# Moving six of eight chunks of one half row's upper partitions onto the lower ones, in a two-layer decode step

## The chip, the cores and the metric

The kernel runs on one core of one Trainium2 chip. Its engines are TensorE (PE in the profile; PEld is its weight load), VectorE (DVE), ScalarE (ACT), GpSimd (POOL) and SyncE (SP). Data is moved by sixteen DMA engines that all queues share. The metric is the time of one execution in microseconds, the median of several runs, on the device.

## What is computed

Two decode layers are run twice over a batch of 2 with one new token each: attention over a cache, then a gated MLP, each behind a layer norm and with a residual.

```python
def _A_ref(x, k_cache, v_cache, wq, wo):
    q = (x @ wq).reshape(B, Sq, H, Dh)...
    scores = jnp.einsum("bhqd,bhkd->bhqk", q, k_cache) * (Dh ** -0.5)
    o = jnp.einsum("bhqk,bhkd->bhqd", softmax(scores), v_cache)
    return o... @ wo
def _B_ref(x, w_gate, w_up, w_down):
    g = jnp.einsum("bsd,df->bsf", x, w_gate)
    u = jnp.einsum("bsd,df->bsf", x, w_up)
    return jnp.einsum("bsf,fd->bsd", _gelu(g) * u, w_down)

x = A_x
x = x + _A_ref(_layernorm(x), A_k_cache, A_v_cache, A_wq, A_wo)
x = x + _B_ref(_layernorm(x), B_w_gate, B_w_up, B_w_down)
x = x + _A_ref(_layernorm(x), A_k_cache, A_v_cache, A_wq, A_wo)
x = x + _B_ref(_layernorm(x), B_w_gate, B_w_up, B_w_down)
```

The batch is 2, the model width D is 576, there are 32 heads of 128 with a cache of 8192 positions, and the MLP width DF is 4608. Everything is float32.

## The kernel before

**Space.** One tile, `space` (line 133), holds 50,176 floats in each of 128 partitions. Nearly all that is loaded goes there: cache parts, and the rows of the weights. A small planner, `Arena` (lines 68 to 119), gives out ranges of it while the program is written: `slots` and `pair` for cache parts, `ring` for pieces of fixed size, and `fit` (line 107) for any width, at the first free place from where the last one ended.

**Order of the loads.** `plan_first`, `plan_mlp` and `plan_second` (lines 324 to 412) put every load into one list, `queue`, in the order in which the work will need them. `pump` (line 148) issues from the head of the list as long as the planner has room. `done` (line 152) frees a range after the last instruction that reads it and pumps again. So loads are written into the program as early as room allows, all on SP's queue (`nc.sync.dma_start`), and the tile framework adds the semaphore waits: for the instructions that last read the range, and for earlier transfers. Transfers take one of eight completion semaphores in turn.

**Order of the engines.** The instructions of each engine stand in the order in which the Python code calls them (`manual_schedule`, line 131). Between engines only the semaphores decide.

**Attention.** Each layer reads 64 pairs of batch and head. VectorE multiplies keys with the query (line 644), GpSimd adds halves (line 661), VectorE reduces (line 664), ScalarE takes the exponential (line 721), and TensorE multiplies with the values (line 762). At the end `project` (lines 807 to 817) multiplies eight groups of wo's rows, one after another as they land; a group has 16 matmuls, for 4 rows and 4 column strips. `add_to_x` (line 520) adds the result to x.

**The second MLP.** `norm` (line 486) centres x and transposes it into `xt`, in which each of nine 32-column blocks holds the 128 entries that belong to one block of weight rows. The gate and up matrices have 576 rows of 4608; each row is cut into two half rows of 2304, which gives 1152 half rows, nine for each of the 128 partitions. `half_rows` (line 221) loads some of the nine for all partitions in one transfer: three transfers of three for gate, then two of three and three of one for up (`GU`, line 305). Row and half fall on partitions so that even and odd partitions hold the two halves.

`all_products` (line 959) multiplies them in that order. For each of the nine there are eight matmuls: the 2304 columns are eight chunks of 288 (HG), of which chunk (v, c) is added up in strip c (32 partitions) of half v of `acc`. `window` (line 938) is the 8-column slice of `xt` that serves as the left operand.

Then `activate` (line 973) works on each half v in turn: a scaled copy on ScalarE (line 976), a transpose, and the GELU and product with up on VectorE and ScalarE, into `hT`. Last come the down products (line 1004): 36 rows per partition, loaded in eight transfers (`down`, line 264), each transfer's products following `IDLE` idle matmuls (`idle_products`, line 524), which compute nothing that is used. `add_to_x` and two stores (line 1019) end the kernel.

Of the kernel before, what the change touches and what calls it, by code (L numbers as in the profile page):

```python
# [9 lines left out]
F32 = mybir.dt.float32  # L10
# [5 lines left out]
P = 128  # L16
B = 2
# [8 lines left out]
HALF = P // 2  # L26

GH = 4
NU = 9
EQ = 512  # L30
HG = DF // 16
PAD = 6
# [9 lines left out]
RING = 5 * SLOT  # L42
END = RING + NPLACE * PLACE
HELD = 5


class Item:
# [75 lines left out]
def decode_layers(ctx, tc, x_in, kc, vc, wq, wo, wg, wu, wd, out):  # L123
    nc = tc.nc
    scale = DH ** -0.5

    consts = ctx.enter_context(tc.tile_pool(name="consts", bufs=1))
# [18 lines left out]
    queue, ready, places = [], {}, {}  # L146

    def pump():
        while queue and queue[0]():
            queue.pop(0)  # L150

    def done(key):
        arena.free(key)
        pump()

    def part_at(at, n):
        return space[:, at:at + n]
# [51 lines left out]
    def weights(key, n, first, transfers):  # L209

        def make():
            at = arena.ring(key, n) if first is None else arena.fit(key, n, first)
            if at is None:
                return False
            t = ready[key] = part_at(at, n)
            transfers(t)
            return True

        queue.append(make)

    def half_rows(key, w, us, first):

        width = w.shape[1] // 2
        rows = w.rearrange("r (s w) -> (r s) w", w=width).rearrange("(p u) w -> p u w", p=P)

        def transfers(t):
            nc.sync.dma_start(t.rearrange("p (u w) -> p u w", w=width), rows[:, us[0]:us[-1] + 1, :])

        weights(key, len(us) * width, first, transfers)

    def of_half(h, k):

        width = wq.shape[1] // 2
        rows = wq.rearrange("r (s w) -> (r s) w", w=width).rearrange("(p u) w -> p u w", p=P)

        def transfers(t):
            for e in range(2):
                nc.sync.dma_start(t[e::2, :], rows[e::2, 2 * k + (h + e) % 2, :])

        weights(("wq", 1, h, k), width, None, transfers)  # L240

    def split_rows(name, w, h, u):

        rows = w[:, DF // 2 * h:DF // 2 * (h + 1)].rearrange("(m r) w -> m r w", r=NU)

        def transfers(t):
            for e in range(2):
                nc.sync.dma_start(t[e::2, :], rows[:, 5 * e + u, :])

        weights((name, 0, h, u), DF // 2, None, transfers)  # L250

    def split_middle(h):

        def transfers(t):
            for g, w in enumerate((wg, wu)):
                for e in range(2):
                    lo, n = DF // 4 * (2 * h + e), DF // 4
                    nc.sync.dma_start(
                        t[e::2, n * g:n * (g + 1)], w[:, lo:lo + n].rearrange("(m r) w -> m r w", r=NU)[:, 4, :]
                    )  # L260

        weights(("gu", 0, h), DF // 2, None, transfers)
# [136 lines left out]
    def plan_mlp(layer):  # L399
        if layer == 0:  # L400
            for h in range(2):
                for u in range(4):
                    split_rows("g", wg, h, u)
                split_middle(h)
                for u in range(4):
                    split_rows("u", wu, h, u)
        else:
            for g, (name, w) in enumerate((("g", wg), ("u", wu))):
                for us in GU[g]:
                    half_rows((name, layer, us[0]), w, us, 0)  # L410
        for rows in DOWN[layer]:
            down(layer, rows)

    plan_first()
    plan_mlp(0)
    plan_second()
    plan_mlp(1)
    pump()


    ident = consts.tile([P, P], F32, name="ident")
# [27 lines left out]
    side = consts.tile([P, 2], F32, name="side")  # L449
# [9 lines left out]

    xt = consts.tile([P, PAD + NU * 32], F32, name="xt")
    nc.vector.memset(xt, 0.0)


    acc = psum1.tile([P, 2, 512], F32, name="acc")
# [13 lines left out]
    def small(p, n):  # L480

        smalls.append(smalls.pop(0))
        return smalls[0][0:p, 0:n]
# [36 lines left out]
    def add_to_x():  # L520
        nc.vector.tensor_add(x, xps, x)  # L521
# [409 lines left out]
    def mlp(layer):  # L931
        split = layer == 0
        rstd = norm(split)
        if split:
            idle_products(3)
        hT = once.tile([P, 2, NI, 2, 2, B], F32, name="hT", tag="xc")

        def window(u, at):

            return xt[:, PAD + 32 * u - at:PAD + 32 * u - at + 4 * B]  # L940

        def split_products(h):

            steps = [(("g", layer, h, u), u, 2, (0,)) for u in range(4)] + [(("gu", layer, h), 4, 1, (0, 1))]
            steps += [(("u", layer, h, u), u, 2, (1,)) for u in range(4)]
            for key, u, sides, gs in steps:
                w = ready.pop(key).rearrange("p (k c w) -> p k c w", c=4, w=HG)
                for k in range(2):
                    g, e = (k, 0) if u == 4 else (gs[0], k)
                    for c in range(4):  # L950
                        nc.tensor.matmul(
                            acc[32 * c:32 * c + 4 * B, h, :HG], window(u, 4 * g + 2 * e), w[:, k, c, :],
                            start=(key == steps[0][0] and k == 0), stop=(key == steps[-1][0] and k == 1),
                        )
                done(key)
                if key != steps[-1][0]:
                    idle_products(1)

        def all_products():

            for g, name in enumerate("gu"):
                for us in GU[g]:
                    w = ready.pop((name, layer, us[0])).rearrange("p (u v c w) -> p u v c w", v=2, c=4, w=HG)
                    for u in us:
                        for v in range(2):
                            for c in range(4):
                                nc.tensor.matmul(
                                    acc[32 * c:32 * c + 4 * B, v, :HG], window(u, 4 * g), w[:, u - us[0], v, c, :],
                                    start=(g == 0 and u == 0), stop=(g == 1 and u == NU - 1),
                                )  # L970
                    done((name, layer, us[0]))

        def activate(v):

            o = once.tile([P, 2, HG], F32, name="o", tag="row")
            nc.scalar.activation(o[:, 0, :], acc[:, v, :HG], AF.Copy, scale=rstd)  # L976
            gu = o[:, 1, :].rearrange("p (i r) -> p i r", i=NI)
            nc.vector.transpose(gu, o[:, 0, :].rearrange("p (m i) -> p i m", i=NI))  # L978
            g = gu[:, :, 0:4]
            a = once.tile([P, NI, 4], F32, name="ga", tag="part")  # L980
            nc.vector.tensor_mul(a, g, g)
            nc.vector.tensor_scalar(a, a, 0.044715, 1.0, op0=ALU.mult, op1=ALU.add)
            nc.vector.tensor_mul(a, a, g)
            nc.scalar.activation(a, a, AF.Tanh, scale=math.sqrt(2.0 / math.pi))
            nc.vector.scalar_tensor_tensor(a, a, 1.0, g, op0=ALU.add, op1=ALU.mult)
            nc.vector.tensor_mul(a, a, gu[:, :, 4:8])
            a, to = a.rearrange("p i (e b) -> p (i e) b", b=B), hT[:, v].rearrange("p i e s b -> p (i e) s b")
            nc.vector.tensor_scalar_mul(to[:, :, 0, :], a, 0.5)
            nc.scalar.mul(to[:, :, 1, :], a, 0.5)

        if not split:
            all_products()
        for v in range(2):
            if split:
                split_products(v)
            activate(v)
        for n, rows in enumerate(DOWN[layer]):
            if n < len(IDLE[layer]):
                idle_products(IDLE[layer][n])
            w = ready.pop(("d", layer, rows[0])).rearrange("p (i c) -> p i c", c=D)  # L1000
            for k, (t, i) in enumerate(rows):
                v, e = divmod(t, 2) if split else (t % 2, t // 2)
                for c in range(4):
                    nc.tensor.matmul(  # L1004
                        xps[32 * c:32 * c + 2 * B, :], hT[:, v, i, e, :, :].rearrange("p s b -> p (s b)"),
                        w[:, k, c * CW:(c + 1) * CW],
                        start=(rows is DOWN[layer][0] and k == 0), stop=(t, i) == (NT - 1, NI - 1),
                    )
            done(("d", layer, rows[0]))
        add_to_x()  # L1010
        if layer == 0:
            idle_products(1)
# [34 lines left out]
```

## Time and profile before

| | |
|---|---|
| time, median of 3 runs | 2686.63 us (2686.4 to 2686.9) |
| profiled execution, first to last instruction | 2685.0 us |
| loaded from memory | 1153.18 MB, 429 GB/s over the span |
| DVE busy | 1806.0 us (67%) |
| POOL busy | 1161.8 us (43%) |
| PE busy | 914.4 us (34%) |
| ACT busy | 163.7 us (6%) |

The profile is of one execution, taken by the hardware. Its page has the busy time of each engine, forty slices of the span with the share of the DMA engines and the clock that TensorE was granted, the DMA queues, the chain of waits that ended last, and the costliest groups of instructions. A row of the timeline has the start and the length in us, the engine, the line of the kernel, the operation, the tile that it writes and those it reads, the shape, the count, and in brackets the idle time ahead of it with what ended that. A matmul in float32 stands in the rows as two instructions. An engine's name with a q is its sequencer, which issues transfers and waits.

### The profile page before, as it was taken

The numbers are of one execution on the slowest core, as the hardware profiler recorded it, in microseconds if no ns is written. First come the engines' busy times: TensorE is split into PE (matmuls) and PEld (weight loads), VectorE is DVE, ScalarE is ACT, GpSimd is POOL, SyncE is SP. The second block draws the span as 40 slices with busy tenths as digits, with TensorE's granted clock in tenths as the row PEclk, the third lists the DMA queues.
The fourth block names the chain that finished last, engine by engine and source line by source line (L and its number), as shares of the span: only waits on it lengthen the run. The fifth ranks groups of instructions, "written<-read, shape, count | busy, mean of one in ns | idle before, by whom it ended". The sixth has DMA issues, their size and how long they took to land. (4 is left out here: it accounts for less than half of the span.)

```text
span 2685.0 us, 17174 instructions
## 1 busy us (share of the span) xinstructions
PE 914.4 (34%) x7150; PEld 305.4 (11%) x7150; DVE 1806.0 (67%) x874; ACT 163.7 (6%) x786; POOL 1161.8 (43%) x261
## 2 busy tenths in 40 slices
PE   1323332332233233334663333233223323332356
PEld 0100010010001000111221101001000100010022
DVE  4876687677667766867037877667766776776640
ACT  0000000000000000000026000000000000000000
POOL 2543454354445444544028455445444543454420
PEclk7656666665666566566986665666566656656678
DMA  9999999999999999999999999999999999999998
GB/s 422 436 436 426 437 432 434 433 434 432 433 431 435 436 428 433 436 428 425 414 418 434 431 431 436 431 434 434 437 428 434 434 435 431 431 434 435 433 421 375
DMA packets 33950, 1154.30 MB, mean 430 GB/s; under 512 B 4152, under 2 KB 4176, under 8 KB 5968
## 3 DMA queue, kind: packets, MB, share of 16 engines
q1 hardware_dynamic: 33832, 1153.19, 99.8%
q8 instruction: 56, 0.92, 0.1%
q14 instruction: 22, 0.18, 0.0%
q10 hardware_dynamic: 40, 0.01, 0.0%
HBM read 1153.18 MB, written 0.00 MB: 429 GB/s over the span
## 5 line engine op out<-in xcount | busy, mean ns | idle before, releaser
L661 POOL TENSOR_TENSOR space<-space 128x3072 f32<-128x3072 f32 (+3 forms) x221 | 1128.6, 5107 | 1263.3 <-DVE space L644 1202.5
L644 DVE TENSOR_TENSOR space<-space,bank 128x6144 f32<-128x6144 f32 (+3 forms) x223 | 1112.7, 4991 | 560.2 <-DMA space<-in_A_k_cache_dram 496.8
L762 PE MATMUL acc<-space,prz 128*8 128x512 f32 x4096 | 594.6, 744 | 199.4 <-DMA space<-in_A_v_cache_dram 195.5
L664 DVE TENSOR_REDUCE S<-space 128x48 f32<-128x3072 f32 (+3 forms) x223 | 569.3, 2553 | 89.9 <-POOL space L661 89.6
L592 PE MATMUL bank<-qsb,pick 4*64 4x128 f32 (+1 forms) x256 | 46.3, 436 | 863.1 <-DVE space L644 853.1
L762 PEld LDWEIGHTS acc<-space,prz 128*8 128x8 f32 x4096 | 119.1, 104 | 616.3 <-issue 410.6
L784 PE MATMUL bank<-of,osb 128*32 128x2 f32 x512 | 40.9, 202 | 324.4 <-DVE osb L777 324.4
L713 ACT ACTIVATE nbs<-bank 128x2 f32<-128x2 f32 (+1 forms) x68 | 11.6, 171 | 1848.2 <-PE bank L698 1801.8
L592 PEld LDWEIGHTS bank<-qsb,pick 4*64 4x64 f32 (+1 forms) x256 | 20.7, 202 | 882.5 <-DVE space L644 863.2
L517 POOL TENSOR_TENSOR rstd<-ve,mhalf 128x1 f32<-128x1 f32 x4 | 2.2, 550 | 168.8 <-DVE ve L515 168.8
L690 PE MATMUL bank<-ident,m 128*1 128x128 f32 x68 | 19.5, 286 | 160.7 <-DVE m L688 160.5
L784 PEld LDWEIGHTS bank<-of,osb 128*32 128x32 f32 x512 | 35.9, 154 | 331.7 <-DVE osb L777 330.5
L978 DVE STREAM_TRANSPOSE o<-o 128x288 f32<-128x288 f32 x4 | 2.8, 691 | 94.5 <-ACT o L976 94.5
L729 PE MATMUL bank<-sums,unit 128*128 128x2 f32 x120 | 35.2, 363 | 87.0 <-ACT prz L721 87.0
L776 DVE TENSOR_TENSOR acc<-acc,diag 128x512 f32<-128x512 f32 x64 | 43.5, 680 | 22.0 <-PE acc L762 22.0
L721 ACT ACTIVATE prz<-S,nbs 64x128 f32<-64x128 f32 (+1 forms) x128 | 50.7, 396 | 17.3 <-POOL prz L711 14.4
L803 ACT ACTIVATE oT<-bank,rinv 32x8 f32<-32x8 f32 x110 | 28.5, 259 | 381.5 <-PE bank L784 380.8
L654 ACT ACTIVATE space<-space 128x128 f32<-128x128 f32 x164 | 48.3, 296 | 23.6 <-DVE space L644 21.7
L698 PE MATMUL bank<-m,unit 1*128 1x2 f32 (+1 forms) x136 | 39.0, 354 | 25.3 <-DVE m L696 25.3
L777 DVE TENSOR_REDUCE osb<-acc 128x128 f32<-128x512 f32 x64 | 44.3, 691 | 2.2
L521 DVE TENSOR_TENSOR x<-bank,x 128x144 f32<-128x144 f32 x4 | 1.2, 308 | 64.1 <-PE bank L1004 40.4
L729 PEld LDWEIGHTS bank<-sums,unit 128*128 128x128 f32 x120 | 30.1, 311 | 92.2 <-ACT prz L721 92.2
(73 smaller groups left out, 427.6 us busy)
## 6 DMA issues: line engine op xcount, KB each, us to landing
space<-in_A_v_cache_dram SPq DMA_DIRECT2D x8, 4096.0 KB
space<-in_A_k_cache_dram SPq DMA_DIRECT2D x6, 4096.0 KB
space<-in_A_wo_dram SPq DMA_DIRECT2D x15, 1152.0 KB
space<-in_A_k_cache_dram SPq DMA_DIRECT2D x15, 1024.0 KB
space<-in_B_w_down_dram SPq DMA_DIRECT2D x9, 1152.0 KB
space<-in_B_w_gate_dram SPq DMA_DIRECT2D x3, 3456.0 KB
space<-in_A_v_cache_dram SPq DMA_DIRECT2D x10, 1024.0 KB
space<-in_A_wq_dram SPq DMA_DIRECT2D x3, 3072.0 KB
```

Of the source, the lines that this page charges most:

```text
L592: nc.tensor.matmul(qb[n][to, :], pick[32 * c:32 * c + 4, r:r + 1].to_broadcast([4, P // it.heads]), qsb[32 * c:32 * c + 4, (h % 4) * DH:(h ...
L644: nc.vector.tensor_tensor(out=u[:, :rows, :], in0=t[:, :rows, :], in1=qb[n].unsqueeze(1).to_broadcast([P, rows, DH]), op=ALU.mult)
L654: nc.scalar.activation(u[:, j, :], u[:, j, :], AF.Copy, accum_out=S[n][:, k * JC + j:k * JC + j + 1])
L661: nc.gpsimd.tensor_tensor(out=half, in0=half, in1=u[:, :r, DH // 2:], op=ALU.add)
L664: nc.vector.tensor_reduce(out=S[n][:, k * JC:k * JC + own_rows(n, k, m)], in_=prod.pop((n, k)), axis=AX.X, op=ALU.add)
L698: nc.tensor.matmul(mT[n][:, :heads], ones[0:1, :], m1[:, :heads], start=True, stop=True)
L721: nc.scalar.activation(pr[at, lo:].rearrange("p (g e) -> p g e", e=4)[:, 0:it.rows // 2:2, :], s[at, :it.rows].rearrange("p (g r) -> p g r ...
L729: nc.tensor.matmul(tot[n][:, :ITEMS[n].heads], ones, rs.pop(n), start=True, stop=True)
L762: nc.tensor.matmul(accumulator(n)[32 * c:32 * c + 8, :], pr[:, at:at + 8], t[g // 4][:, g % 4 * 4:g % 4 * 4 + 4, :].rearrange("p j d -> p ...
L776: nc.vector.tensor_tensor(out=q, in0=q, in1=diag.unsqueeze(2).to_broadcast([P, 4, DH]), op=ALU.mult)
L777: nc.vector.tensor_reduce(out=t, in_=q.rearrange("p r d -> p d r"), axis=AX.X, op=ALU.add)
L784: nc.tensor.matmul(po[lo:lo + 32, i, :], t[:, i::GH], of, start=True, stop=True)
```

## The change

Of the second MLP's up matrix, the ninth half row of each partition is loaded and multiplied in another way.

- `lower_rows` replaces `half_rows` for it. One transfer loads the last two chunks (576 columns) for all 128 partitions. The first six chunks (1728 columns, CUT = 6) are loaded by eight transfers, each to eight of the lower 64 partitions, four apart. Each brings two runs per partition: the partition's own, and that of the partition 64 above it. The second run lies 4 columns further on than the first one's end. The place in `space` is 4040 columns wide; before it was 2304.
- `move_down` copies the upper partitions' block of `xt` for this half row down to the lower ones: a matmul with a part of the identity, and a copy on ScalarE into four new columns at the end of `xt`. It is called ahead of all products.
- `last_products` replaces the eight matmuls of the ninth up half row. Each of the first six chunks is multiplied in two matmuls over the lower 64 partitions, one for each run; the last two chunks as before over all 128.

```diff
+CUT = 6
...
+    def lower_rows(key, w, u, cut, first):
+
+        width = w.shape[1] // 2
+        rows = w.rearrange("r (s w) -> (r s) w", w=width).rearrange("(q u) w -> q u w", u=NU)[:, u, :]
+        moved = rows.rearrange("(s a j i) w -> a i j s w", s=2, a=2, i=4)
+
+        def transfers(t):
+            nc.sync.dma_start(t[:, 2 * (cut + 4):], rows[:, cut:])
+            to = t[:HALF, :2 * (cut + 4)].rearrange("(a j i) (s w) -> a i j s w", a=2, i=4, s=2)
+            for a in range(2):
+                for i in range(4):
+                    nc.sync.dma_start(to[a, i, :, :, :cut], moved[a, i, :, :, :cut])
+
+        weights(key, width + cut + 8, first, transfers)
...
-                    half_rows((name, layer, us[0]), w, us, 0)
+                    if name == "u" and us[0] == NU - 1:
+                        lower_rows((name, layer, us[0]), w, us[0], CUT * HG, 0)
+                    else:
+                        half_rows((name, layer, us[0]), w, us, 0)
...
-    xt = consts.tile([P, PAD + NU * 32], F32, name="xt")
+    xt = consts.tile([P, PAD + NU * 32 + 2 * B], F32, name="xt")
...
+        def move_down():
+
+            first = small(P, 2 * B)[:HALF]
+            at = PAD + 32 * (NU - 1)
+            nc.tensor.matmul(first, ident[HALF:, HALF:], xt[HALF:, at:at + 2 * B], start=True, stop=True)
+            nc.scalar.copy(xt[:HALF, at + 32:at + 32 + 2 * B], first)
+
+        def last_products():
+
+            key = ("u", layer, NU - 1)
+            w, side = ready.pop(key), CUT * HG + 4
+            for n in range(8):
+                v, c = divmod(n, 4)
+                to = acc[32 * c:32 * c + 4 * B, v, :HG]
+                if n >= CUT:
+                    at = 2 * side + (n - CUT) * HG
+                    nc.tensor.matmul(to, window(NU - 1, 4), w[:, at:at + HG], start=False, stop=True)
+                    continue
+                for s in range(2):
+                    at = s * side + n * HG
+                    nc.tensor.matmul(
+                        to, window(NU - 1 + s, 4)[:HALF], w[:HALF, at:at + HG], start=False, stop=(s == 1)
+                    )
+            done(key)
...
         def all_products():
...
+                    if name == "u" and us[0] == NU - 1:
+                        last_products()
+                        continue
...
         if not split:
+            move_down()
             all_products()
```

## The prediction

> **What bounds the kernel now.** I read the page first, then the chain of waits over the last 90 us, then the timeline of that stretch, and last the order of instructions and waits in the two built programs.
>
> The page's slices of DMA business and the chain's shares:
>
> ```profile
> DMA  9999999999999999999999999999999999999998
> ...
> DMA 28%; DVE 13%; POOL 3%; PE 0%; issue 0%; ACT 0%; POOLq 0%; SPq 0%
> ```
>
> The sixteen DMA engines are full in every slice but the last, so the kernel is limited by the bytes that it loads. At the end, where the change sits, the chain of waits (start us, us, what) holds almost nothing but loads:
>
> ```profile
> 2603.68 49.37 DMA space<-in_B_w_up_dram
> ...
> 2653.07 27.34 DMA space<-in_B_w_down_dram
> 2680.41 0.04 issue
> 2680.45 0.67 PE bank L1004 x16
> ...
> 2681.16 0.47 PE bank L1004 x8
> ```
>
> The up weights land until 2653.07 and the down weights until 2681.16; behind the last piece stand only 0.47 us of TensorE and the final sum. TensorE works in the gaps, as its timeline shows:
>
> ```profile
> 2603.66 2.10 PE L812 MATMUL bank<-space,oT 128*4 128x144 f32 x32 [0.67 <-DMA space<-in_A_wo_dram]
> ...
> 2606.54 1.63 PE L812 MATMUL bank<-space,oT 128*4 128x144 f32 x32 [0.78 <-DMA space<-in_A_wo_dram]
> 2608.24 0.31 DVE L521 TENSOR_TENSOR x<-bank,x 128x144 f32<-128x144 f32 x1 [16.86 <-PE bank L812]
> ...
> 2610.57 0.69 DVE L511 STREAM_TRANSPOSE xt<-xc 128x288 f32<-128x288 f32 x1
> ...
> 2614.77 4.56 PE L967 MATMUL acc<-space,xt 128*8 128x288 f32 x48 [5.19 <-DMA space<-in_B_w_gate_dram]
> ...
> 2617.84 38.34 SPq L271 DMA_DIRECT2D space<-in_B_w_down_dram  x8
> ...
> 2622.88 3.10 PE L967 MATMUL acc<-space,xt 128*8 128x288 f32 x48 [3.55 <-DMA space<-in_B_w_gate_dram]
> ...
> 2653.10 0.61 PEld L967 LDWEIGHTS acc<-space,xt 128*8 128x8 f32 x16 [0.36 <-DMA space<-in_B_w_up_dram]
> 2655.88 0.60 PEld L967 LDWEIGHTS acc<-space,xt 128*8 128x8 f32 x16 [2.17 <-DMA space<-in_B_w_up_dram]
> 2655.88 1.16 PE L967 MATMUL acc<-space,xt 128*8 128x288 f32 x16 [1.62 <-DMA space<-in_B_w_up_dram]
> ...
> 2657.16 0.50 ACT L976 ACTIVATE o<-acc,rstd 128x288 f32<-128x288 f32 x1 [79.92 <-PE acc L967]
> ...
> 2659.82 0.23 ACT L989 ACTIVATE hT<-ga 128x36 f32<-128x36 f32 x1 [0.49 <-DVE ga L986]
> ```
>
> The seventh and eighth output projections (L812), the norm, and the products with gate and up (L967) each run as their weights land, between 2603.66 and 2657.04, hidden under the loads. SP issues the down weights from 2617.84 on, so the queue never runs dry.
>
> **What the change does in the built program.** The diff alone would be a matter of 2 us of bytes. The waits that the tile framework put in decide. Of SP's list (first lines are those of the two files; DMAHW0 to 7 are the eight completion semaphores that transfers take in turn):
>
> ```
> before  DMACopy space<-in_B_w_up_dram   128x2304  [waits DMAHW1, PE]
>         DMACopy space<-in_B_w_down_dram 128x5184  [waits DMAHW2, PE]
> after   DMACopy space<-in_B_w_up_dram   128x576   [waits DMAHW1, PE]
>         DMACopy space<-in_B_w_up_dram   8x2x1728  [waits all eight, PE]
>         DMACopy space<-in_B_w_up_dram   8x2x1728  x7
>         DMACopy space<-in_B_w_down_dram 128x5184  [waits all eight, PE]
> ```
>
> and of TensorE's, at the seventh projection:
>
> ```
> before  Matmult bank<-space,oT 4x144  [waits DMAHW0]
> after   Matmult bank<-space,oT 4x144  [waits all eight]
> ```
>
> with no DMA wait any more before the gate and up products. The counts in these waits say which transfers are meant. The first 8-partition transfer waits until everything ahead of it has landed, the 128x576 piece included. The first down transfer waits until all eight have landed, and for the ninth gate product. The seventh projection, which before waited only for its own wo rows, waits for all eight small transfers. So the projections, the norm and all products, which ran from 2603.66 on under the loads, now start when the ninth up half row has come in whole. That is the step I take as decisive.
>
> **Part by part.** Everything ahead stands as before: SP's list is the same up to the 128x576 piece, whose issue waits, as that of the whole half row did, for the semaphore of the last wo rows (used at 2606.54 above) and for a projection, both far ahead of its turn in the queue.
>
> (1) The 128x576 piece. u's eighth half row lands at 2653.10 (PEld row above). The piece has 288 KB; the last down piece has the same size and came 2681.16 - 2680.45 = 0.71 us after the one before it. So it lands at 2653.81.
>
> (2) The eight transfers of 108 KB, 864 KB together. Now the queue is empty, so each such step pays a whole round trip. The only drained transfer near is the output's, in the timeline and in SP's waits:
>
> ```profile
> 2682.00 0.64 SPq L1019 DMA_DIRECT2D out_dram<-x  x1
> ```
>
> ```profile
> SPq L1043 <- DMA out_dram<-x: 1.3, 1, 1.3
> ```
>
> 0.64 + 1.3 = 1.94 us from issue to landing for 2.2 KB. For the data, the row of ACT's queue (packets, MB, share):
>
> ```profile
> q10 hardware_dynamic: 40, 0.01, 0.0%
> ```
>
> ACT issued eight loads of x on two partitions and one store from four. Forty packets are 8 x (2 + 2) + (4 + 4), one data packet and one completion per partition. So I take a transfer of eight partitions to occupy eight engines, half of the page's mean of 430 GB/s:
>
> ```profile
> DMA packets 33950, 1154.30 MB, mean 430 GB/s; under 512 B 4152, under 2 KB 4176, under 8 KB 5968
> ```
>
> 884,736 B / 215 GB/s = 4.1 us. Bounds: 2.1 us if all sixteen engines share it, 8 x 1.94 = 15.5 us if each transfer pays its own round trip. SP queues them without waits between, which speaks for 4.1. With 0.2 us for the chained waits: 2653.81 + 1.94 + 4.1 + 0.2 = 2660.05.
> [...]
>
> (3) Two projections. The sixth projection ended ahead of 2603.66, so TensorE has then been idle for 56 us. The granted clock in three stretches (columns: us, busy PE, PEld, DVE, ACT, POOL, clock, DMA share, GB/s):
>
> ```profile
> 2603.60:2605.80 2.20, 2.10 (x32) 1.01 (x32) 0.00 (x0) 0.00 (x0) 0.00 (x0) 0.50 1.01 431
> ...
> 2614.70:2617.80 3.10, 3.03 (x28) 1.15 (x32) 0.00 (x0) 0.00 (x0) 0.00 (x0) 0.50 1.02 437
> ...
> 2622.80:2626.00 3.20, 3.10 (x48) 1.22 (x48) 0.00 (x0) 0.00 (x0) 0.00 (x0) 1.00 0.99 423
> ```
>
> At 0.50 a projection is 2.10 us, and after an idle stretch about 3 us pass at 0.50 before 1.00 comes. Two at 2.10, with 0.1 for the waits: 2664.35.
>
> (4) Sum and norm, from 0.07 ahead of the DVE row at 2608.24 to the end of the transpose at 2611.26: 3.1 us; 2667.45. Then the added move_down matmul, held at 0.3 us by the small one of L690; its copy on ACT runs beside the products, which need it only at the end:
>
> ```profile
> 2574.99 0.27 PE L690 MATMUL bank<-ident,m 128*1 128x128 f32 x1 [2.89 <-DVE m L688]
> ```
>
> 2667.75. The wider xt (4 more columns in one memset at the start) costs nothing: it lies ahead of the first load's landing.
>
> (5) Seventeen half rows, 272 instructions, now without a pause. At full clock 48 take 3.10 us, the last 0.2 of which is drain paid once: some 17.0 us. The slow start costs 4.56 - 3.10 = 1.5 (both rows above; nothing to 3.4 as bounds). 2686.25.
>
> (6) The ninth half row: 14 matmuls for 8, the moved ones over 64 rows and the same 288 columns, so none is cheaper. Before, ACT began 2657.16 - 2655.88 = 1.28 us after it. The first half's four extra matmuls add 0.5 (at 3.10 us per 24) to 1.5 (if the two of a pair, which go to the same output rows, can't overlap); I take 0.8. 2688.3. The activations of the first half then take 2660.05 - 2657.16 = 2.9: 2691.2. The second half's come under the first down piece.
>
> (7) The down products. Before, each waited for its load. Now SP issues the first down transfer about 3.07 us after the products start (2617.84 - 2614.77), at 2670.8. With 1.94 and the 25.28 us that these loads took (2655.88 to 2681.16), the last one lands at 2698.0. TensorE gets to the first at 2691.2, so it runs through:
>
> ```profile
> 2666.01 1.89 PE L526 MATMUL bank<-prz,ident 128*4 128x256 f32 x8
> 2668.35 2.39 PE L1004 MATMUL bank<-space,hT 128*4 128x144 f32 x72 [0.45 <-DMA space<-in_B_w_down_dram]
> 2670.55 1.03 PE L526 MATMUL bank<-prz,ident 128*4 128x256 f32 x4
> 2671.69 1.41 PE L1004 MATMUL bank<-space,hT 128*4 128x144 f32 x40
> ...
> 2674.87 1.16 PE L1004 MATMUL bank<-space,hT 128*4 128x144 f32 x32 [0.93 <-DMA space<-in_B_w_down_dram]
> 2675.85 0.59 PE L526 MATMUL bank<-prz,ident 128*4 128x256 f32 x2
> 2676.95 0.92 PE L1004 MATMUL bank<-space,hT 128*4 128x144 f32 x24 [0.51 <-DMA space<-in_B_w_down_dram]
> ...
> 2680.45 1.14 PE L1004 MATMUL bank<-space,hT 128*4 128x144 f32 x24 [0.48 <-DMA space<-in_B_w_down_dram]
> ```
>
> 2.39 + 1.89 + 2.39 + 1.03 + 1.41 + 1.03 + 1.16 + 0.59 + 0.92 + 0.92 + 1.14 = 14.9, less 0.5 where drains overlap the next: 14.4. [...] TensorE ends at 2705.6. Before, it ended at 2681.16 + 0.47 = 2681.63. What follows (final sum, output) is the same. **The sum: +24.0 us.** The profiled span of 2685.0 becomes 2709.0; the median shown is 1.6 us above that span, and I take what lies around it as unchanged: 2686.63 + 24.0 = **2710.6 us**.
>
> **The rivals.**
> (a) Only SP's two drains count, because TensorE's wait is met early (if it turned out to mean older transfers). Then the end is set by loads: 2660.05 + 0.2 + 1.94 + 25.28 = 2687.5 in place of 2681.16, +6.3, **2692.9**. Against it: the counts on TensorE are the ones that the eight small transfers bring about. Chance 0.04.
> (b) On the other side, one mechanism: the engines end unevenly, and the late ones are relieved.
>
> ```profile
> 2670.00:2674.00 4.00, 3.83 (x73) 2.05 (x64) 0.00 (x0) 0.00 (x0) 0.00 (x0) 1.00 0.99 406
> ...
> 2679.00:2680.00 1.00, 0.92 (x24) 0.54 (x24) 0.00 (x0) 0.00 (x0) 0.00 (x0) 1.00 0.43 173
> ```
>
> The DMA share falls from 0.99 to 0.43 in the last microseconds: some engines are done while others still load. If the late ones are those of the upper partitions, they lose three quarters of the 2.78 us that the ninth half row took (2653.10 to 2655.88): -2.1, **2684.5**. It decides only if the small transfers queue up behind the rest without a wait. Both lists say the opposite. Chance 0.02. [...] The rows show uneven ends but not which engines.
> (c) The small transfers run one by one: +24.0 + 11.4 = **2722.0**, the bound of step 2. For it: nothing but that no such transfer is shown. Chance 0.05.
>
> **How the numbers follow.** The forecast has 0.87, the last 0.02 is for what I haven't thought of. Within it, step 2 is uncertain by -2 to +1, the clock in step 5 by -1.5 to +1.9, pairs in step 6 by -0.3 to +0.7, the drains in steps 5 and 7 by 1 either way. Together I give 2705 to 2716, some 0.82 of all cases. 0.2% (5.4 us) is about what a measurement of this kernel can tell from no change. Forecast, (c) and (a) (by a hair) lie above it: slower 0.96, within 0.2% 0.03, faster by more 0.01; (b) is within it.
>
> **What would show it.** In the changed profile: SP's eight small issues in a row near 2654 and the first down issue near 2671; TensorE idle from about 2603 to 2660, then a solid block of L967's successor without DMA waits until about 2688; DMA slices near the end that are half empty; and a chain whose last 45 us are TensorE and not DMA. I am wrong if the seventh projection still runs near 2603.7, or if the down products still wait for loads.

## The result, and the profile after

The changed kernel takes **2712.06 us** (median of 4 runs, 2711.96 to 2712.94) where the kernel before takes 2686.62 (4 runs beside it): 25.4 us slower, ratio 1.0095 (95% interval 1.0081 to 1.0109). Its profiled execution, the longest of the four (2712.94), spans 2711.1 us, 26.1 more than that of before. Forecast were 2710.6 and slower.

The page's DMA slices first. Before, the last one stood at 8 and all others at 9; now the last one is half empty:

```profile
DMA  9999999999999999999999999999999999999995
```

The chain of waits over the last 110 us (start us, us, what) says where the time lies:

```profile
2606.88 47.23 DMA space<-in_B_w_up_dram
...
2654.25 0.87 SPq L243
2655.17 0.71 SPq L243
...
2659.13 0.67 SPq L243
2659.84 3.51 DMA space<-in_B_w_up_dram
...
2663.44 4.06 PE bank L831 x64
...
2670.87 18.30 PE acc L1014 x272
2689.17 2.05 PE acc L998 x24
...
2691.91 0.51 ACT o L1023
...
2694.86 2.39 PE bank L1052 x72
...
2705.52 2.27 PE bank L1052 x64
2707.81 0.31 DVE x L540
```

Up to 2654 it is loads, as before. Then come eight issues of SP one after the other, the landing of the last small transfer at 2663.35, and from there to the end hardly anything but TensorE: the two projections that used to run at 2603.66 (L831, L812 before), the norm, all gate and up products (L1014, L998), and the down products. The timeline's row of the projection names what TensorE waited for, and how long:

```profile
2663.44 4.02 PE L831 MATMUL bank<-space,oT 128*4 128x144 f32 x64 [60.99 <-DMA space<-in_B_w_up_dram]
```

It reads wo rows, which had landed by 2606.82 (the chain's wait for the last of them ends there), and stood 61 us for an up transfer. What the loads did meanwhile is in the windows (us, busy PE, PEld, DVE, ACT, POOL, clock, DMA share, GB/s):

```profile
2650.00:2654.00 4.00, 0.00 (x0) 0.00 (x0) 0.00 (x0) 0.00 (x0) 0.00 (x0) 0.50 0.32 130
2654.00:2656.00 2.00, 0.00 (x0) 0.00 (x0) 0.00 (x0) 0.00 (x0) 0.00 (x0) 0.50 0.12 28
2656.00:2660.00 4.00, 0.00 (x0) 0.00 (x0) 0.00 (x0) 0.00 (x0) 0.00 (x0) 0.50 0.40 114
...
2664.00:2672.00 8.00, 5.27 (x80) 2.91 (x76) 2.41 (x8) 0.16 (x1) 0.55 (x1) 0.71 0.01 2
```

```profile
2673.50 7.30 SPq L287 DMA_DIRECT2D space<-in_B_w_down_dram  x8
```

From 2650 on the queue runs dry, since nothing is issued behind the ninth half row, and between 2664 and 2672 almost nothing is loaded: by SP's row, the last one above, the first down transfer goes out at 2673.50, when the ninth matmul of the gate products is done.

### The profile page after: what moved, and what is told of

It reads as the page before. It is cut to its first block, busy times and chain, and to the rows that moved or that the text cites. A ratio compares the mean times of both kernels' runs of the same rounds, so it can differ in the third digit from the quotient of the medians.

```text
span 2711.1 us, 17217 instructions
## 1 busy us (share of the span) xinstructions
PE 901.1 (33%) x7164; PEld 303.8 (11%) x7164; DVE 1806.0 (67%) x874; ACT 163.8 (6%) x787; POOL 1161.5 (43%) x261
## 5 line engine op out<-in xcount | busy, mean ns | idle before, releaser
L740 ACT ACTIVATE prz<-S,nbs 64x128 f32<-64x128 f32 (+1 forms) x128 | 50.7, 396 | 17.3 <-POOL prz L730 14.4
L717 PE MATMUL bank<-m,unit 1*128 1x2 f32 (+1 forms) x136 | 39.1, 355 | 25.4 <-DVE m L715 25.4
L831 PE MATMUL bank<-space,oT 128*4 128x144 f32 x512 | 20.3, 306 | 70.5 <-DMA space<-in_B_w_up_dram 61.0
```

What stands on the lines that cost most here:

```text
L717: nc.tensor.matmul(mT[n][:, :heads], ones[0:1, :], m1[:, :heads], start=True, stop=True)
L740: nc.scalar.activation(pr[at, lo:].rearrange("p (g e) -> p g e", e=4)[:, 0:it.rows // 2:2, :], s[at, :it.rows].rearrange("p (g r) -> p g r ...
```

## The experiments

**Theory.** The time is lost by the waits that the tile framework gave for the form of the small transfers: TensorE's seventh projection and SP's first down transfer wait for all eight, and the first of them for everything ahead. **Rivals.** The eight 8-partition transfers cost it by themselves (slow issue, or data over eight engines only, as the prediction had estimated), or the doubled matmuls do; and rival (b) of the prediction, that the layout in itself relieves late engines and only its waits hide this.

| kernel | what it has | median us | against before beside it | ratio, 95% interval |
|---|---|---|---|---|
| changed | all | 2712.06 | +25.4 | 1.0081 to 1.0109 |
| e1_waits_pe | all waits, nothing moved | 2706.36 | +19.7 | 1.0055 to 1.0089 |
| e2_waits_sp | SP's two drains, nothing moved | 2693.36 | +6.7 | 1.0015 to 1.0034 |
| e3_no_gap | all moved, one drain | 2692.48 | +5.8 | 1.0011 to 1.0030 |
| e4_two_wide | all moved, two transfers, plain waits | 2693.72 | +7.1 | 1.0017 to 1.0036 |
| e5_one_run_each | all moved, 16 transfers, plain waits | 2694.66 | +8.1 | 1.0018 to 1.0041 |
| e6_adjacent | all moved, adjacent partitions, plain waits | 2694.02 | +7.5 | 1.0016 to 1.0036 |
| e7_four_of_16 | all waits, 4 transfers | 2709.50 | +23.0 | 1.0071 to 1.0101 |
| e8_cut_2 | all waits, a third moved | 2712.40 | +25.9 | 1.0081 to 1.0111 |
| e9_early | all moved, issued early | 2688.51 | +1.9 | 0.9997 to 1.0015 |
| e10_early_2 | a third moved, issued early | 2687.19 | +0.5 | 0.9992 to 1.0010 |

### The waits alone: e1 and e2

e1 is the kernel before with one small transfer more, whose data nobody reads:

```diff
...
+            nc.sync.dma_start(t[:, :width], rows)
+            to = t[:HALF, width:].rearrange("(a j i) (s w) -> a i j s w", a=2, i=4, s=2)
+            nc.sync.dma_start(to[0, 0, :, :, :432], few[0, 0, :, :, :432])
...
```

(`few` is cut from the same rows, with the same strides.)

> Nothing is moved: the ninth up half row loads and multiplies as before. Added is one 8-partition transfer of the changed kernel's form (partitions four apart, two runs four columns apart, 27 KB, read by nobody) behind it. It brings all the wide waits: it waits for everything ahead of it, the first down transfer waits for it, and TensorE's seventh projection waits for it. Theory (the waits cost the time): it lands at 2655.9 + 0.2 + 1.9 = 2658.0, the seventh projection starts there, and what follows takes as long as in the changed kernel, where 47.7 us pass from that projection to the end of the span, less 1.2 for the pairs and the move: span 2704.5, time 2706 (2703 to 2708), +19. Rival (the eight small transfers or the paired products cost it): 2686.6 to 2689.

2706.36. Its timeline on TensorE:

```profile
2658.38 4.02 PE L828 MATMUL bank<-space,oT 128*4 128x144 f32 x64 [56.23 <-DMA space<-in_B_w_up_dram]
2663.39 0.62 PE L510 MATMUL bank<-apart,same 128*128 128x24 f32 x2 [0.99 <-DVE apart L506]
2665.76 20.22 PE L983 MATMUL acc<-space,xt 128*8 128x288 f32 x288 [1.75 <-DVE ve L531]
```

One transfer of 27 KB that nobody reads holds TensorE for 56 us, and with SP's drains beside it costs 19.7 of the 25.4. No byte of the half row is moved, and no product is doubled. The remaining 5.7 are the changed kernel's own: its last small transfer lands 5.1 us later (2663.35 against 2658.24 here), and from the first product to the first activation pass 21.04 us (2670.87 to 2691.91) against 20.35 (2665.76 to 2686.11), 0.7 for the pairs.

e2 differs from it by the length of the two runs only, and by that TensorE's wait is gone:

```diff
-            nc.sync.dma_start(to[0, 0, :, :, :432], few[0, 0, :, :, :432])
+            nc.sync.dma_start(to[0, 0, :, :, :864], few[0, 0, :, :, :864])
```

> As e1, but with runs of 864 columns, by which TensorE's seventh projection gets no wait for the added transfer, and only SP's two drains are left: the added transfer waits for everything ahead of it, and the first down transfer waits for the added one. Theory: the queue runs dry for two round trips less what the loads hide: added transfer landed 2658.0, first down data 2.1 later in place of 2655.9: +4.3, 2690.9 (2689 to 2692.5). Rival (waits cost nothing): 2686.6.

2693.36, and TensorE's eighth projection ends at 2608.90, as its rows land. So SP's two drains cost 6.7 us by themselves, and the wait on TensorE adds 13 to make e1's 19.7. The 6.7 are 2.4 more than I had expected, just above my range. The windows of e2, and one of before ahead of them, show what I left out:

```profile
2648.00:2656.00 8.00, 6.38 (x80) 2.36 (x76) 0.00 (x0) 0.00 (x0) 0.00 (x0) 0.79 1.03 437
```

```profile
2650.00:2652.00 2.00, 2.00 (x36) 0.77 (x32) 0.00 (x0) 0.00 (x0) 0.00 (x0) 0.89 0.64 272
2652.00:2654.00 2.00, 1.84 (x32) 0.62 (x28) 0.00 (x0) 0.00 (x0) 0.00 (x0) 1.00 0.51 217
2654.00:2656.00 2.00, 0.44 (x8) 0.00 (x0) 0.00 (x0) 0.00 (x0) 0.00 (x0) 1.00 0.16 69
2656.00:2658.00 2.00, 1.95 (x21) 0.86 (x22) 0.14 (x1) 0.50 (x1) 0.00 (x0) 1.00 0.06 17
2658.00:2660.00 2.00, 0.91 (x5) 0.17 (x2) 1.53 (x6) 0.23 (x1) 0.00 (x0) 1.00 0.28 66
2660.00:2662.00 2.00, 0.00 (x0) 0.00 (x0) 1.43 (x5) 0.62 (x2) 0.00 (x0) 1.00 0.85 280
```

The half row lands at 2656.00 by its semaphore, but the share is 0.64 in 2650 to 2652 already, then 0.51 and 0.16: I read this as engines that have done their part, with nothing behind it, while others still load. Before, the share was 1.03 through these microseconds. So the drains cost here the round trip (2.46 us from the added transfer's issue at 2656.15 to its landing) and, by this reading, on top the time by which the engines were apart. Against 430 GB/s the six rows lack 3.3 MB (158 + 213 + 361 + 413 + 364 + 150, times 2 us), or 7.7 us of full rate, beside the 6.7 that the run lost.

### Everything moved, but not these waits: e3, e5

e3 puts the second run straight behind the first one; by that TensorE's wait goes, and the small transfers wait for their lanes only. The first down transfer still waits for all eight.

```diff
-            nc.sync.dma_start(t[:, 2 * (cut + 4):], rows[:, cut:])
-            to = t[:HALF, :2 * (cut + 4)].rearrange("(a j i) (s w) -> a i j s w", a=2, i=4, s=2)
+            nc.sync.dma_start(t[:, 2 * cut:], rows[:, cut:])
+            to = t[:HALF, :2 * cut].rearrange("(a j i) (s w) -> a i j s w", a=2, i=4, s=2)
...
```

> The changed kernel with the two runs of each moved partition next to each other instead of four columns apart. TensorE and the small transfers have only the waits of their own lanes; the first down transfer still waits for all eight. Everything moved, the eight issues, the pairs and the moved rows of x stay. Theory: seven of the eight are queued ahead; the last lands 2657 to 2658, first down data 2659 to 2660 in place of 2655.9: +3 to +4.2, 2690 (2688.5 to 2691.5). Rival (transfers or products cost it): 2705 to 2712.

2692.48, a microsecond above the range and 20 below the changed kernel, with the same bytes, the same places but for four to eight columns, the same eight issues and the same pairs. SP's row has them spread over 40 us, each as an earlier transfer lands:

```profile
2614.59 40.03 SPq L243 DMA_DIRECT2D space<-in_B_w_up_dram  x8
2657.95 4.42 SPq L287 DMA_DIRECT2D space<-in_B_w_down_dram  x8
```

The first down transfer goes out at 2657.95. What it misses by is, as in e2, probably the engines' spread: over 2650 to 2652 the share is 0.63 already, at 245 GB/s. The rival of the small transfers and that of the pairs, which expected 2705 or more, fall as causes of the 25.4 us.

e5 loads the two runs with a transfer each, so that all the wide waits go and there are sixteen transfers instead:

```diff
-                    nc.sync.dma_start(to[a, i, :, :, :cut], moved[a, i, :, :, :cut])
+                    for s in range(2):
+                        nc.sync.dma_start(to[a, i, :, s, :cut], moved[a, i, :, s, :cut])
```

> The changed kernel with each of the eight transfers split in two, one run of 1728 columns each: sixteen transfers of 8 partitions four apart, and none of the wide waits: TensorE's seventh projection and products wait for their own loads, each transfer for the one eight before it, the first down transfer for the ninth of the sixteen. Bytes, places, pairs and move are as in the changed kernel. Theory (the wide waits cost most, SP's slow issue of 8-partition transfers the rest): the first seven go ahead of the last 128x576 piece, nine are issued after it at 0.7 us, so the down data begins some 6 us late: 2693 (2690 to 2697). Rival (small transfers of this kind or the pairs cost the time by themselves): 2712 or more, since there are twice as many.

2694.66, in the range. SP's rows of it by line (duration min/median/max in ns, first and last start), and the timeline's:

```profile
L244 SPq DMA_DIRECT2D space<-in_B_w_up_dram x16: 623/624/755, 2615.0 to 2659.5; - x16
```

```profile
2660.24 4.30 SPq L288 DMA_DIRECT2D space<-in_B_w_down_dram  x8
```

Nothing waits widely here, yet the down transfers start at 2660.24: with eight completion semaphores in turn, nine of the sixteen can't be issued before the 128x576 piece has landed, and SP takes 0.62 us for each.

### How the moved rows are loaded: e4, e6

e4 brings them as two transfers of 64 partitions with plain waits, which should have left nothing to pay:

```diff
+            for s in range(2):
+                at = s * (cut + 4)
+                nc.sync.dma_start(t[:HALF, at:at + cut], rows[s * HALF:(s + 1) * HALF, :cut])
```

> The moved rows come as two transfers of 64 partitions in place of eight of 8, with plain waits everywhere; the pairs and the move stay. Theory: nothing left to pay, 2686.6 (2685.5 to 2687.5). [...] Rival (paired products cost it): 2695 and more.

2693.72: theory missed, by 6.2 us above its range. The rival of the pairs, with 2695 and more, came nearest, but it isn't the cause: e4's chain ends in loads, with 0.47 us of TensorE behind the last one, and e9 below has the same pairs at 2688.51. The first down transfer is issued early, at 2631.06, and the engines don't stop:

```profile
2650.00:2652.00 2.00, 2.00 (x32) 0.55 (x23) 0.00 (x0) 0.00 (x0) 0.00 (x0) 0.90 0.98 251
...
2654.00:2656.00 2.00, 0.00 (x0) 0.00 (x0) 0.00 (x0) 0.00 (x0) 0.00 (x0) 1.00 1.13 252
...
2660.00:2662.00 2.00, 1.12 (x2) 0.10 (x2) 0.00 (x0) 0.00 (x0) 0.00 (x0) 0.50 0.92 235
```

The share is about 1, but the rate is 251 and 235 GB/s, where before had 437 over 2648 to 2656. So the engines are occupied and move little more than half as much, for some 14 us: 209 to 308 GB/s in the rows from 2648 to 2662, 244 on average, at shares of 0.92 to 1.16. What lowers the rate, no run shows. The moved 864 KB at half rate would take only some 4 us (884,736 B / 215 GB/s); whether the transfers queued beside them were held up too, no run separates.

e6 keeps eight transfers of 8 partitions and the gap, but takes partitions next to each other, which gives plain waits:

```diff
+            to = t[:HALF, :2 * (cut + 4)].rearrange("(a j) (s w) -> a j s w", a=8, s=2)
+            near = rows.rearrange("(s a j) w -> a j s w", s=2, a=8)
+            for a in range(8):
+                nc.sync.dma_start(to[a, :, :, :cut], near[a, :, :, :cut])
```

> The changed kernel with eight transfers of 8 partitions next to each other in place of four apart, two runs with the gap kept. No wide waits. Theory: only the eighth transfer is issued after the 128x576 piece and the first down transfer waits for the first of them alone: 2688 to 2690, below the 2692.5 of e3_no_gap, which kept one drain. If writes to few neighbouring partitions get in each other's way, as packets took double their time in e4_two_wide, up to 7 more: 2695. Rival (any 8-partition transfers cost it): 2705 to 2712.

2694.02, within the 2695 allowed for writes that get in each other's way and above theory's 2688 to 2690. The windows are partly of the kind of e4's (in an execution of 2692.32 us):

```profile
2646.00:2650.00 4.00, 2.32 (x20) 0.75 (x24) 0.00 (x0) 0.00 (x0) 0.00 (x0) 0.50 0.90 256
...
2656.00:2658.00 2.00, 0.15 (x4) 0.00 (x0) 0.00 (x0) 0.00 (x0) 0.00 (x0) 1.00 0.88 221
```

At 0.90 busy they moved 256 GB/s, where e3 moved 245 at 0.63. So eight neighbouring partitions were the slower destination here, and four apart the faster form; but four apart with two runs that don't join is the form that gets the wide waits. Not all of e6's loss is of this kind: over 2654 to 2656 the share falls to 0.39, as the first down transfer goes out only at 2656.48. The two parts are not separated.

### The small transfers' stretch: e7 and e8

Step 2 had taken 9.2 us (2654.11 to 2663.35) and not the 6.2 forecast. e7 issues four transfers of 16 partitions, e8 moves a third of the bytes in eight transfers:

```diff
-            for a in range(2):
-                for i in range(4):
-                    nc.sync.dma_start(to[a, i, :, :, :cut], moved[a, i, :, :, :cut])
+            for i in range(4):
+                nc.sync.dma_start(to[i, :, :, :cut], moved[i, :, :, :cut])
```

```diff
-CUT = 6
+CUT = 2
```

> The changed kernel with four transfers of 16 partitions four apart in place of eight of 8; all wide waits stay. In the changed kernel the stretch from the landing of the 128x576 piece to that of the last small transfer took 9.2 us, of which 5.6 are seven issues of about 0.8. Theory (SP's issue sets that stretch): four issues fewer, 3 us less: 2709 (2708 to 2710.5). Rival (the data over few engines sets it): unchanged, 2712.

> The changed kernel with 2 of 8 chunks moved in place of 6: still eight transfers of 8 partitions with all the waits, each with 36 KB in place of 108, behind a 128x1728 piece in place of 128x576. Theory (waits and issue): the piece lands 1.4 us later and the last small transfer 0.5 us sooner after its issue, with four pairs fewer: 2711.5 to 2713, as the changed kernel. Rival (bytes moved set the price): a third of 25.4: 2695; if only step 2 goes by bytes, 2707 to 2709.

2709.50 and 2712.40, both as the theory had it. In e7's chain the stretch is 2653.74 to 2660.33, 6.6 us; it ends so:

```profile
2653.88 0.64 SPq L242
2654.57 0.59 SPq L242
2655.16 0.35 issue
2655.51 0.55 SPq L242
2656.06 0.06 issue
2656.12 4.21 DMA space<-in_B_w_up_dram
```

Four issues fewer are 2.6 us less in time. In e8 the stretch is 7.9 us (2655.02 to 2662.94): the seven starts take 5.66 us as they took 5.59 in the changed kernel, but with a third of the bytes the last transfer lands 2.12 us after its issue and not 3.51:

```profile
2660.82 2.12 DMA space<-in_B_w_up_dram
```

The time is no less, as the last piece ahead of them is longer by what they are shorter. So SP's issuing sets most of that stretch, and the data some 1.4 us at its end.

### Issued early enough: e9 and e10

If only waits and a dry queue cost time, the moved layout should come out even when its transfers are ahead of their turn. e9 is e3 with four of the eight ahead of the second triple of up half rows and four behind it; e10 is e9 with `CUT = 2`.

```diff
...
+        weights(key, width + cut, first, lambda t: some(0))
+        queue.append(lambda: some(1))
+        queue.append(rest)
+        one, two, three = queue[-3:]
+        before = queue[-6:-3]
+        queue[-6:] = [one, before[0], two, *before[1:], three]
...
```

(`some(a)` issues four of the eight, `rest` the 128x576 piece.)

> The changed kernel without the gap, as e3_no_gap, and with the small transfers issued earlier: four ahead of the second triple of up half rows, four behind it, the 128x576 piece last. The waits that the first down transfer has for them are then over before its turn, so the queue should not run dry. Everything moved, pairs and move stay. Theory (only waits and a dry queue cost time): 2686.6, that is within 2 of before (2685 to 2688.5). Rival b of the prediction (the late engines are those of the upper partitions and are relieved): 2684.5. Rival (8-partition transfers cost time even when nothing waits for them): 2690 and more.

> [...] Theory: 2686.6 (2685 to 2688). Rival b: between 2684.5 and 2686. Rival of the transfers: 2689 and more.

2688.51 and 2687.19 beside 2686.65: +1.9 (e9, 0.01 above its range) and +0.5, both intervals of the ratio holding 1. In e9's chain the last 25 us are loads again:

```profile
2641.64 15.19 DMA space<-in_B_w_up_dram
...
2656.85 25.35 DMA space<-in_B_w_down_dram
...
2682.95 0.47 PE bank L1060 x8
```

So 23.5 of the 25.4 us go when the same bytes lie in the same layout but nothing waits for them widely at a bad moment. Most of e9's 1.9 is a dip that is left, since its first down transfer still goes out only at 2651.36. Over 2640 to 2656 it moved 0.6 MB less than the kernel before, 1.4 us at full rate; the lowest row:

```profile
2648.00:2652.00 4.00, 2.74 (x24) 0.90 (x28) 0.00 (x0) 0.00 (x0) 0.00 (x0) 0.50 0.86 361
```

And nothing is gained: no version was faster than the kernel before. Rival (b) expected 2684.5 of e9, and 1.4 more for the dip would be 2685.9, well below the 2688.51 measured; in neither run does moving load to the lower partitions bring the end forward. Which of the engines are the late ones, and which partitions they write, no row shows.

## Why the prediction was right

The mechanism was the one forecast, and e1 shows it apart from all else. By its steps:

1. The 128x576 piece: 2653.81 forecast, 2654.11 measured.
2. **The small transfers: the term that was mis-sized.** Forecast 6.2 us, measured 9.2 (2654.11 to 2663.35). I added one round trip (1.94) and the data over eight engines (4.1, an estimate: no run shows how many engines a small transfer takes), and took SP's eight issues to hide behind the data. SP's row by line (min/median/max ns):

```profile
L243 SPq DMA_DIRECT2D space<-in_B_w_up_dram x8: 666/673/868, 2654.3 to 2659.8; - x8
```

   Seven starts apart make 5.6 us, then 3.5 for the last one. The row to see it from stood in my fence: the store of 4 partitions took 0.64 us to issue; eight of these are 5.1 us, more than the data's 4.1. I used it for a single latency and didn't multiply it. A small count of partitions alone didn't make an issue slow here, though: e6's eight, next to each other, took 0.27 each. The data, on which I had put the step, shows in the last landing only, with 1.4 of its 3.5 us (e8).
3. Two projections: 4.18 measured with the waits (2663.35 to 2667.53); 4.3 forecast.
4. Sum, norm and move_down: 3.34 (2667.53 to 2670.87) against 3.4.
5. Seventeen half rows: 18.30 against 18.5, the stretch at 0.50 included. My 17.0 in it was wrong by its own rows: 272/48 times 2.9 and 0.2 of drain are 16.6 (48 in 3.10 us and 16 in 1.16, both at 1.00, are 0.061 each and 0.2 over). That leaves 1.7 for the clock and not 1.5; the windows have it at 0.50 from 2671.2 until 2674.6. The two errors nearly cancel, by luck. The 3 us at 0.50 were those of one stretch only: in the kernel before, the products from 2639.30 to 2645.20 ran at 0.51 throughout.
6. The ninth half row to the activation: 2.74 (2689.17 to 2691.91) against 2.08. The pairs' share was right, 0.7 by e1 against 0.8, and over 64 rows none was cheaper: 0.085 us each (24 in 2.05) against 0.067 for those over 128 (272 in 18.30); the plain run of products was some 0.6 longer than my sum had it, steps 5 and 6 taken together without the pairs (20.35 in e1 against 17.0 + 1.5 + 1.28). The activations took 2.95, against 2.9.
7. The down products: 12.95 (2694.86 to 2707.81) against 14.4. I had taken 0.5 off 14.9 for overlapping drains; run through without waits they came to some 1.9 less (14.9 less 12.95), and the rows overlap: seven idle products from 2697.06 last 1.67, to 2698.73, and the next group starts at 2698.36. Loads had landed before TensorE got there, as forecast.

In sum +0.3 + 3.0 - 0.1 - 0.1 - 0.2 + 0.7 - 1.4 = +2.2 on the forecast end of 2705.6, and TensorE ended at 2707.81. That two errors of opposite sign, in steps 2 and 7, made the total better than its parts was luck. The median is only 1.5 above the forecast, as the profiled execution was 0.9 longer than the median.

Rival (a), only SP's drains, was priced at 2692.9. e2, which is that case with one transfer, took 2693.36, but not by my working: I had the drain too cheap (no engine spread) and the eight transfers are not in it. Rival (c) fell with the row of step 2: the issues follow each other at 0.7 us, with no round trip between.

What stays open: why a gap of four columns, or runs of 432 columns and not of 864, bring the wait on TensorE. The built programs show that it is there, and the runs what it costs; the rule by which the framework decides was not found. It isn't that their places meet: the place of the added transfer begins at column 11520 of `space` in e1 and e2 and ends at 12392 and 13256, and the seventh projection's rows begin at 13824 in both. How the cost of e4 and e6 divides is open as well.

## What to carry to other kernels

Where a framework places the waits, read the built program's wait lists around a new transfer before its bytes are counted: one transfer of an awkward form, read by nobody, cost 19.7 us. A load that must come last should have the plainest destination there is; if its form is awkward, issue it early, when what waits for it has time: in e9 that took back 23.5 of the 25.4 us. And where the queue runs dry, count every issue on SP (0.67 us for each of the eight here), and the time that the engines are apart, not only one round trip (with both, e2 lacked 7.7 us of full rate).

## What the runs showed of the hardware

- How long SP took to issue a transfer went with its destination: 0.67 us at the median for 8 partitions four apart (`L243` above), 0.62 with one run each (e5), 0.55 to 0.64 for 16 four apart (e7). For 8 partitions next to each other it was 0.27 (e6, first row), and 0.33 for the 128x576 piece in the changed kernel (second row):

```profile
L243 SPq DMA_DIRECT2D space<-in_B_w_up_dram x8: 272/272/338, 2614.7 to 2656.1; - x8
2606.88 0.33 SPq L239 DMA_DIRECT2D space<-in_B_w_up_dram  x1
```

- A DMA share near 1 was not the full rate: around its 64-partition transfers e4 moved 235 to 252 GB/s at shares of 0.92 to 1.13 (its rows above), the kernel before 437 at 1.03.
- By the shares, the DMA engines didn't end their part of a load together. In e2 the share fell to 0.64 (272 GB/s) four to six microseconds before the half row's landing at 2656.00, where the kernel before had 1.03 (437 GB/s), and the first drain paid for that.
